# Queries loaded four tokens to a row, in a linear-attention and Fourier-mixing kernel

## The chip, the cores and the metric

The kernel runs on one core of a Trainium2 chip. The metric is the device time of one execution in microseconds (us); lower is better. A core has TensorE (PE, with its weight loads PEld), VectorE (DVE), ScalarE (ACT), GpSimd (POOL) and SyncE (SP), and sixteen DMA engines that all queues share.

## The reference

Four batches, eight heads, 768 tokens, a head dimension of 48. First comes attention with a decaying state per head (r is the query, k the key, v the value), then a mixing of the result by Fourier transforms over tokens and features, a normalisation and two dense layers (384 to 1,536 to 384).

```python
for t in range(S):
    cur = einsum('bhd,bhe->bhde', u * k_t, v_t)
    y[:, :, t] = einsum('bhd,bhde->bhe', r_t, state + cur)
    state = w[None, :, :, None] * state + einsum('bhd,bhe->bhde', k_t, v_t)
...
u = x + real(fft(fft(x, axis=1), axis=2))      # x: y with the heads side by side
un = (u - mean(u)) / sqrt(var(u) + 1e-06)
return u + relu(un @ w_ch1) @ w_ch2
```

## The kernel before

**Tiles.** The tokens of a batch are cut into six chunks of 128, so there are 24 chunks, numbered 0 to 23, six to a batch. A chunk has 128 tokens on the partitions.

**Attention of a chunk (`attend`).** `load` brings k, r and v from memory into float32 tiles: kr holds k in its first half and r in its second, eight heads of 48 each; vt holds v. Each of the three is one DMA with rows of 48 numbers (192 bytes). KR (L302, DVE) multiplies k and r by a table of decays by token, wtab, and writes them as bfloat16 into a tile whose heads are padded from 48 to 64 columns. For chunks below `TURNED` = 15, eight transposes on PE (tp, L316) turn KR, and one copy KRT, on ACT (L325) or DVE (L326), brings the result out of PSUM; from chunk 15 on a DMA transpose does both. From KRT come PR (key times query, L327), the scores A (L337), which are masked (AC and MA, on ACT with POOL, or on DVE with the table mtri), the state S (u at L369, times the decay WD), and yd, which collects the chunk's result; X is the chunk's output.

**Fourier part and dense layers.** When a batch's six X are there, HH, EO and XF fold them, matmuls with the cosine and sine tables te and hid do the transforms, UF and UB hold the sum and its normalised form, and UNT its transpose. A batch has two halves of three blocks. For each half `mlp1` makes twelve matmul groups hp (L678) with the eviction HT on ACT (L683) or DVE (L686), and `mlp2` makes three output blocks mo of twelve matmuls (L698), in two half blocks of six; osb (L705) adds the input and SP stores the block.

**Order.** Nothing is scheduled on the chip: each operation is an entry with a number, a choice of engines and a due priority, and `ORDER`, a long list of numbers written into the file, tells in which order they are emitted and (".1") that the second engine of the choice is taken. Each engine works through its own entries in that order and waits where its data is late. The list interleaves the dense layers of one batch with the attention of the next. At the start PE gets fillers (idle, L203), matmuls on zeros.

**Queues.** SP issues every load of k, r (but that of chunk 0, which ACT issues) and v, the tables te, hid, ident, mtri, the DMA transposes and the stores. POOL issues the two dense weights in three parts each. kr and vt have four buffers.

**Start.** DVE zeroes the five KR tiles whole, the states, and WD, which is a table of 128 x 384 numbers in two versions. ACT takes the logarithm of w (lw) and makes the three wtab by exponentials, for the three places that a chunk can have in its half batch.

Of the kernel before, what the change touches and what calls it, by code (L numbers as in the profile page):

```python
# [27 lines left out]
def _tables():  # L28
# [18 lines left out]
    mtri = np.triu(np.ones((128, 128)), 1)  # L47
    ident = np.eye(128)
    return [np.ascontiguousarray(x.astype(bf)) for x in (te, hid, mtri, ident)]
# [43 lines left out]
118 93 135 90 108 114 110 91 137 101 117 109 95 116 111 94 102 92 98 138 136 105 0 97 129 1 107 140 96 2 112 3 132 99 113 104 4 119 5 106 120 141 6  # L93
103 121 7 139 115 122 8 212 9 124 143 10 123 214 125 142 100 11 144 215 12 13 230 14 15 146 126 217 134 127 131 213.1 232 216 218 147 222 133 224 220
233.1 16 219 225.1 17 223.1 18 149 226.1 221 235 231 130 228 234 238.1 227 150 236 240 252 19 241.1 20 21 145 229 237 128 254 239.1 242 152 22 243.1
244.1 23 255 24 148 274 246.1 245 25 247.1 257 256 209 292 276 260.1 258 264 153 277 26 248 27 249 28 29 261.1 151 259 265 253 294 278 279 295 250 262
30 266 282.1 283.1 31 154 32 280 33 251 268 267 275 263 297 210 281 211 269 284 298.1 296 155 286 314 285.1 692 287.1 699 685 156 686 293 288.1 693
948 316 300 299.1 157 290 289 302 317 700 291 301 160 304 270 303.1 318 319 305.1 306.1 158 947 706 315 707 322.1 323.1 320 308.1 307 271 309.1 273
272 324 311 687 321 708 325.1 326.1 694 701 310 328.1 327 159 313 329.1 312 695 331 702 161 330 703 688 333 689 332 696 949 697 690 704 709 691 698.1
710 711 705 34 712.1 713.1 334 715 162 721 335 716 722.1 717 727 723.1 336 163 728 729 344 718 35 36 730.1 724 735 337.1 739 353 737 736 740.1 339 738  # L100
719.1 714 953 340.1 341.1 725.1 720.1 164 741 338 753 954 742 743 726.1 950 346 342 165 754 747 755 744 969 748 343 749 167 756 761 970 750.1 765 168
762 731.1 763 766 975 764 745.1 732.1 370 977 751.1 746.1 1007 976.1 978 372 752.1 1008.1 757.1 973 373.1 347 971 733.1 758.1 974 352 979 166 972 957
345.1 734 980.1 348 1005 169 371 354 1006 388 350 170 349 958 362 959 363.1 355.1 989 172 960 406 357 990 390 171 358.1 389 359.1 963 360 173 391.1
955 964 361 965 351 956 174 1003 392 966 356 375 1004 374 176 380 981 378.1 376 951 381 983 433 177 982.1 407 398 377 379.1 759.1 967 984 179 432 364
968 393 180 365 399.1 995 396.1 394.1 397.1 952 434 996 395.1 416 961 366 417.1 435.1 1001 962 760 368 367 436 437 1002 369 408 438.1 440 439.1 382
175 993 441 409.1 383 991 384 994.1 178 985 992.1 386 454 411 385 412.1 414 413.1 986 415 387 456 987 182 400 457 1033 472 183 401 490 1034 181 410
455 459 1035 402 474 185 460.1 462 997 473.1 404 475 458 186 403 998 463 405 1036 508 418 184 492 419 491 999 420 464 1045 188 461.1 465.1 476 988
422.1 421 525 477 423.1 187 482 442 424 483.1 1009 425 1000 443 493 426 190 500 1046 427 478 193 480 428 1010 444 1047 510 431 446.1 445 501 1021 509
479 1011 1048 447.1 526 196 494 517 449 466 495 448 467 430 1022 451 498.1 496 1012 450 518.1 429 527 453 771 452 767 768 1023 468 769 772 773 770
499.1 534 189 775 497 470.1 774 469 191 776 572.1 777 471.1 779 783 780 778 781 511 484 192 782 512 481 535 485 785 513 486 515.1 516.1 194 791 784.1  # L110
786 797 787 514 792.1 1024 488.1 798 799 487 793.1 529 788.1 806 800 195 794.1 807.1 818 489.1 550 819.1 808.1 805 519 812 571 820.1 37 813 520 810.1
814 197 521 580 38 198 532 789 811.1 523.1 809.1 815 522 39 821.1 524.1 588 826 530 502 40 551 581 533 503 816.1 1013 801 199 1037 528 552 817.1 1014
790 504 802 1017 795 1038 1015 822.1 1018.1 506 505 796 573 1039 589 531 823.1 507 1016 1019 605 1040 536 1020 1049 200 824.1 1065 803 1050 606.1 597
607 825 804 1077 1066 598 537 1025 1078 1067 553 1026 201 538 1053 1068 614 554 1054 203 540 615 1027 555.1 557 556.1 539 1043 1028 574 204 1063 558
1044.1 575 541 1064 206 1029 578 542 1061 576 590 608 559 543 1030 1041 560 1062 609 561 1042.1 207 1031 610 202 544 563 1079 1032 622 1073 1080 1055
1074 205 545 1075 1056 546 1069 547 208 1076 639 562 624 1057 564 579 664 612 1070 623 565 592 611 1071 1051 548 1072 582 1058 566 1052 641 549 583
595 567 568 1093 569 570 1059 584 1094 1060 625 586 827 828 577 1095 829 839 840 830 596 841 1096 593.1 594.1 585 835 640 613 836 842.1 837 665 831
832 587 833 1081 834 838.1 843 845 844 1082 846 847 848.1 849.1 857 1083 631 858 616 850.1 859 632.1 1084 851 866 666 852 853 617 860 872 618 867 626
868 873 854 878 629.1 627.1 874 620 648 869 865 619 879 1117 880 875 855.1 881.1 1118 621 886 870.1 856.1 642 628.1 882.1 633 871.1 1105 667 634 861.1
883.1 630.1 635 1106 862.1 863.1 1119 876.1 637 591 1120 636 864 877.1 884.1 1085 638 1101 885 1086 1107 599 1102 668 649 1108 600 1121 601 669.1 671  # L120
670.1 1145 1122 1087 603 1146 602 1091 1088 672 604 643 1092 650 646.1 644.1 647.1 1097 651 652 1113 645.1 1098 1109 1114 654 653 1111 1110 655 1103
1112 656 673 1104 657 1099 674 1089 675 1100.1 1115 1090 658 677 1135 1116 659 676 1141 1136 678 660 679 1142 680 662 682 1129 663 681 661 684 1130
683 1143 887 888 1144 1131 889 891 892 890 893 1132 899 900 894 901 895 896 902.1 897 1125 898 903 1151 1126 904 905 1152 911 906 907 912.1 917 913.1
908.1 1127 918 919 1147 1128 914.1 926 920.1 1148 1139 927 928 925 932 1140 938 933 934 929 1149 939 940 1153 935 930.1 941.1 909 1154 946 1150 931.1
915 936.1 910 916 1133 942.1 1155 937.1 1137 921 1134 1156 943.1 1157 1138 922 1161 1158 1175 944.1 1162 945 1187 1176 1173 1188 1193 923 1174.1 1199
1194.1 1197 924 1200 1217 1198 1207 1218 1163 1208 1223 1164 1169 1224 1123 1170.1 1211 1124 1181 1212 1177 1182 1178 1195 1179 1189 1196 1180 1190
1221 1191 1209 1222.1 1192 1205 1210.1 1171 1206 1219 1172 1183 1220 1185 1184 1233 1186 1159 1237 1160 1234 1238 1235 1236 1201 1239 1240 1165 1166
1202 1167 1168 1225 1203 1204 1213 1229 1226 1214 1227 1228 1230 1215 1216 1231 1232
# [8 lines left out]
def kernel(  # L137
# [18 lines left out]
    te_n, hid_n, mtri_n, id_n = _tables()  # L156
# [6 lines left out]
    mtri = cp.tile([128, 128], BF16, name="mtri")  # L163
    wrow = cp.tile([128, DM], F32, name="wrow")
# [7 lines left out]
    wtab = [cp.tile([128, 2, DM], F32, name=f"wtab{i}") for i in range(3)]  # L172
    lwc = cp.tile([128, NP], F32, name="lwc")
    wdec = cp.tile([128, NP], F32, name="wdec")
    WD = [cp.tile([128, NP, 2, D], F32, name=f"WD{i}") for i in range(2)]
# [16 lines left out]
    TURNED = 15  # L192
# [16 lines left out]
    def prelude():  # L209
        def dve(ns, fn, r, w, pri):  # L210
            op(w, "DVE", ns + MEMSET, fn, r=r, w=[w], pri=pri)
# [4 lines left out]
        op("wrow", "ACT", 430, lambda: nc.scalar.dma_start(out=wrow, in_=w.rearrange("h d -> (h d)").partition_broadcast(128)),  # L216
# [18 lines left out]
        for i in range(NB):  # L235
            dve(490, lambda i=i: nc.vector.memset(KRs[i], 0.0), [], ("KR0", i), -895 + i if i < 3 else -745 + i)
        dve(60, lambda: nc.vector.memset(eps_t, 1e-6 * DM * DM), [], "eps", -800)
        dve(60, lambda: nc.vector.memset(UW, 0.0), [], "UW0", -800)
        for i in range(2):
            dve(380, lambda i=i: nc.vector.memset(WD[i], 0.0), [], ("WD0", i), -800 + 60 * i)  # L240
            dve(140, lambda i=i: nc.vector.memset(XFs[i][:, :, :, 4 * CH:], 0.0), [], ("XF0", i), -700)
# [3 lines left out]
        act(520, lambda: nc.scalar.activation(lw, wrow, Act.Ln), ["wrow", "lntab"], "lw", -895)  # L245
        for j in range(3):
            act(600, lambda j=j: nc.scalar.activation(wtab[j][:, 0, :], lw, Act.Exp, scale=ncol[:, j:j + 1]),
                ["lw", "ncol"], ("wt", j, 0), -894 + 50 * j)
            act(600, lambda j=j: nc.scalar.activation(wtab[j][:, 1, :], lw, Act.Exp, scale=icol[:, j:j + 1]),
                ["lw", "icol"], ("wt", j, 1), -893 + 50 * j)  # L250
# [41 lines left out]
    def attend(i):  # L292
# [20 lines left out]
        def transposes():  # L313
            for s in range(2):
                for p in range(NP):
                    nc.tensor.transpose(tp()[:, s, p, :], KR()[:, s, p, :], ident)  # L316
# [467 lines left out]
```

## Time and profile before

| what | value |
|---|---|
| runs shown | 182.89, 180.6, 182.84 us; median 182.84 |
| profiled execution | 182.89 us, span on the chip 180.9 us |
| PE busy | 164.0 us (91% of the span) |
| DVE busy | 141.4 us (78%) |
| ACT busy | 117.3 us (65%) |
| POOL busy | 46.8 us (26%) |
| loads of k, r and v | 24 each of 192 KB, 4.3, 4.1 and 4.1 us from issue to landing (median) |

The busy times are of one execution and overlap one another. They are means over a span whose parts differ, so the rows in 40 slices and the windows say more than the shares. "Landing" is the moment when the last part of a transfer has arrived.

### The profile page before, as it was taken

The page shows a single profiled execution, that of the slowest core. Times are in us where ns is not written, and L with a number is a line of the kernel's source. Part 1 is how long each engine was busy: PE and PEld are TensorE (multiplying, and loading weights), DVE is VectorE, ACT ScalarE, POOL GpSimd, SP SyncE. Part 2 cuts the span into 40 slices and gives each one's busy share as a digit, 9 for nine tenths or more (in the row PEclk, how much of TensorE's full clock was granted, in tenths as well). Part 3 has the DMA queues.
Part 4 walks back from the last instruction along what each step waited for, and adds up shares of the span by engine and source line. Part 5 has one row for each costly group of instructions (what it writes and reads, how often), then busy time and mean ns, then how long its engine had stood idle before and what let it go on. Part 6 is the DMA issues. An engine that isn't in the chain of part 4 may idle for free.

```text
span 180.9 us, 4299 instructions
## 1 busy us (share of the span) xinstructions
PE 164.0 (91%) x1627; PEld 107.0 (59%) x1628; DVE 141.4 (78%) x320; ACT 117.3 (65%) x278; POOL 46.8 (26%) x66
## 2 busy tenths in 40 slices
PE   4889897989999897779889999999999999999991
PEld 1345476656676665448456566776667756666650
DVE  7699998999999878999997999997697862231312
ACT  2979892999994257449998943498744798432000
POOL 6033342033263432273423608014210000000000
PEclk9999999999999999999999999999999999999999
DMA  3999999999999799799999894284001260020223
GB/s 94 207 198 209 265 225 211 183 185 177 201 195 213 146 190 221 179 235 231 178 213 197 170 223 125 67 185 135 3 2 46 75 144 1 4 87 0 87 87 130
DMA packets 97828, 26.79 MB, mean 148 GB/s; under 512 B 92432, under 2 KB 97168, under 8 KB 97808
## 3 DMA queue, kind: packets, MB, share of 16 engines
q1 hardware_dynamic: 94480, 23.77, 62.1%
q0 software_dynamic: 2144, 2.36, 8.0%
q10 hardware_dynamic: 1184, 0.39, 0.9%
q8 instruction: 12, 0.20, 0.5%
q14 instruction: 8, 0.07, 0.1%
HBM read 20.03 MB, written 4.72 MB: 137 GB/s over the span
## 4 chain that ended last, share of the span: by engine, by line
PE 49%; DVE 26%; DMA 10%; issue 4%; ACT 4%; SPq 4%; DVEq 0%
PE mm L678 21%; PE mm L698 16%; DMA kr<-in_r_dram 8%; PE mm L546 4%; DVE KR L302 4%; DVE MA L349 3%; DMA vt<-in_v_dram 2%; DVE PR L327 2%; PE mm L586 2%; DVE XF L508 2%; SPq L283 2%; DVE EO L489 2%; DVE X L435 1%; PE A_ps L337 1%; DVE HH L495 1%
## 5 line engine op out<-in xcount | busy, mean ns | idle before, releaser
L678 PE MATMUL mm<-UNT,W 128*128 128x384 bf16 x288 | 52.9, 326 | 0.7 <-DVE HT L686 0.5
L698 PE MATMUL mm<-W,HT 128*128 128x384 bf16 x288 | 50.7, 326 | 0.5 <-DMA W<-in_moe_w_ch_dram 0.5
L683 ACT ACTIVATE HT<-mm 128x384 bf16<-128x384 f32 x81 | 38.6, 493 | 12.2 <-PE mm L678 11.8
L698 PEld LDWEIGHTS <-HT 128*128 128x128 bf16 x288 | 27.1, 98 | 17.5 <-DMA W<-in_moe_w_ch_dram 0.9
L678 PEld LDWEIGHTS <-W 128*128 128x128 bf16 x288 | 26.5, 97 | 16.8 <-issue 1.3
L414 POOL TENSOR_TENSOR TT<-V,DE 128x384 bf16<-128x384 bf16 x19 | 19.7, 1035 | 47.4 <-ACT DE L412 42.4
L705 DVE SCALAR_TENSOR_TENSOR osb<-mm,rstd,UF 128x384 f32<-128x384 f32 x24 | 14.6, 612 | 17.8 <-PE mm L698 17.8
L302 DVE TENSOR_TENSOR KR<-kr,wtab 128x768 bf16<-128x768 f32 x24 | 23.9, 998 | 3.3 <-DMA kr<-in_r_dram 2.9
L346 POOL TENSOR_SCALAR_AFFINE_SELECT MA<-AC 128x512 bf16<-128x512 bf16 x26 | 19.4, 753 | 25.1 <-ACT AC L344 22.6
L344 ACT CAST AC<-A_ps 128x512 bf16<-128x512 f32 x26 | 15.0, 590 | 3.7 <-PE A_ps L337 3.3
L203 PE MATMUL mm<-zero 128*128 128x512 bf16 x40 | 12.9, 439 | 2.6 <-DVE zero L219 2.5
L349 DVE TENSOR_TENSOR MA<-A_ps,mtri 128x512 bf16<-128x512 f32 x22 | 14.8, 682 | 0.2 <-PE A_ps L337 0.2
L310 ACT CAST V<-vt 128x384 bf16<-128x384 f32 x20 | 10.2, 519 | 5.7 <-DMA vt<-in_v_dram 5.6
L555 ACT CAST TT<-mm 97x386 bf16<-97x386 f32 x11 | 6.1, 601 | 11.7 <-PE mm L546 11.7
L546 PE MATMUL mm<-te_t,XF 128*128 128x193 bf16 x99 | 11.5, 247 | 2.3 <-DVE XF L508 1.2
L619 ACT ACTIVATE lw<-UF,sm 128x384 f32<-128x384 f32 x18 | 11.1, 617 | 1.6 <-DVE UF L599 1.4
L546 PEld LDWEIGHTS <-XF 128*128 128x128 bf16 x120 | 9.8, 98 | 3.9 <-DVE XF L508 2.3
L327 DVE TENSOR_TENSOR PR<-KRT 128x512 bf16<-128x512 bf16 x24 | 11.7, 495 | 0.0
L337 PE MATMUL A_ps<-KRT 64*128 64x128 bf16 x192 | 10.0, 219 | 1.7 <-DVE MA L349 1.1
L686 DVE TENSOR_SCALAR HT<-mm 128x384 bf16<-128x384 f32 x15 | 7.9, 550 | 3.9 <-PE mm L678 3.8
L435 DVE TENSOR_TENSOR X<-yd_ps,TT 128x384 bf16<-128x384 f32 x16 | 8.8, 548 | 2.5 <-PE yd_ps L426 2.5
L599 DVE SCALAR_TENSOR_TENSOR UF<-mm,X 128x384 f32<-128x384 f32 x19 | 10.0, 555 | 0.9 <-PE mm L586 0.7
(90 smaller groups left out, 231.3 us busy)
## 6 DMA issues: line engine op xcount, KB each, us to landing
kr<-in_k_dram SPq DMA_DIRECT2D x24, 192.0 KB, 4.3
vt<-in_v_dram SPq DMA_DIRECT2D x24, 192.0 KB, 4.1
out_dram<-osb SPq DMA_DIRECT2D x24, 192.0 KB, 1.9
kr<-in_r_dram SPq DMA_DIRECT2D x23, 192.0 KB, 4.1
W<-in_moe_w_ch_dram POOLq DMA_DIRECT2D x6, 384.0 KB, 6.9
te_t<-te_c SPq DMA_DIRECT2D x1, 579.0 KB, 5.1
hid_t<-hid_c SPq DMA_DIRECT2D x1, 288.0 KB, 3.7
wrow<-in_w_dram ACTq DMA_DIRECT2D x1, 192.0 KB, 3.8
```

Source lines behind the costliest of these rows:

```text
L203: op("idle", "PE", 216, lambda: nc.tensor.matmul(z(), lhsT=zero[:, 0:128], rhs=zero, start=True, stop=True), r=["zero"], w=[("idle", len(s ...
L302: op(("KR", i), "DVE", 960, lambda: nc.vector.tensor_tensor(out=KR().rearrange("t s p (a d) -> t (s p) a d", a=2)[:, :, :, 0:D], in0=kr(). ...
L327: op(("PR", i), "DVE", 410, lambda: nc.vector.tensor_tensor(out=PR(), in0=KRT()[:, 0], in1=KRT()[:, 1], op=AluOp.mult), r=[("KRT", i)], w= ...
L344: op(("AC", i, a), "ACT", 590, lambda: nc.scalar.copy(AC(), A_ps[a]()), r=[("A", i)], w=[("AC", i, a)], new=[AC], use=[A_ps[a]], pri=pri, ...
L346: op(("MA", i, a), "POOL", 630, lambda: nc.gpsimd.affine_select(out=MA[a](), in_=AC(), pattern=[[0, NP], [1, 128]], base=0, channel_multip ...
L349: port=True, other=[("DVE", 680, False, lambda: nc.vector.tensor_tensor(out=MA[a](), in0=A_ps[a](), in1=mtri.unsqueeze(1).to_broadcast([12 ...
L414: op(("TT", i), "POOL", 830, lambda: nc.gpsimd.tensor_tensor(out=TT(), in0=V(), in1=DE().unsqueeze(2).to_broadcast([128, H, D]), op=AluOp. ...
L546: nc.tensor.matmul(fp()[:, par, :], lhsT=lhsT[:, g * CH:g * CH + 128], rhs=rhs, start=(nb == 0 and par == 0), stop=(nb == last and par == ...
L678: nc.tensor.matmul(hp(), lhsT=W1[:, dt, ft * 128:(ft + 1) * 128], rhs=UNT()[:, :, dt, :], start=(dt == 0), stop=(dt == 2))
L683: op(("HT", hf, ft), "ACT", 495, lambda: nc.scalar.activation(out=HT()[:, ft, :], in_=hp(), func=Act.Relu, scale=-1.0), r=[("hp", hf, ft)] ...
L698: nc.tensor.matmul(mo(), lhsT=HT()[:, ft, j * 128:(j + 1) * 128], rhs=W2[:, ft, :], start=(ft == 0), stop=(ft == 11))
L705: op(("osb", hf, j), "DVE", 620, lambda: nc.vector.scalar_tensor_tensor(out=osb(), in0=mo(), scalar=rstd()[:, j:j + 1], in1=UF()[:, j, :], ...
```

## The change

1. The queries of chunks 0 to 14 (`PACKED` = 15) are loaded with four consecutive tokens of a head in one row of 192 numbers (768 bytes). The partition is then a head pair and a group of four tokens, x = 32 g + p, and the row holds four tokens for each of the two heads of a pair. Two DMAs do it, one for the even and one for the odd heads.
2. Such queries need their own decay table (`rtab`): tok, a small table of token numbers, is loaded, multiplied by the logarithms of w in the new layout (`lw2`, loaded by one more DMA), and exponentiated. It replaces the query half of wtab for these chunks; the full table stays for chunks 15 to 23.
3. KR is made in two halves: KK for the keys, KR for the queries. The copy out of PSUM is in two halves too: KT for the keys, and KRT for the queries, which puts the tokens back in order while it writes (every fourth element). Each half has its own choice of ACT or DVE.
4. Only the padding of the KR tiles is zeroed, and WD shrinks to 128 x 8 numbers that are read with a broadcast.
5. `ORDER` is a new list, for the new entries, and with it the places of many operations and their engines change: of the first-layer evictions HT 32 are on DVE (15 before) and 64 on ACT (81 before); there are 50 fillers (41 before).

```diff
-    TURNED = 15
+    TURNED, PACKED, RD = 15, 15, 560
...
-            dve(490, lambda i=i: nc.vector.memset(KRs[i], 0.0), [], ("KR0", i), ...)
+            dve(180, lambda i=i: nc.vector.memset(
+                KRs[i].rearrange("t s p (a d) -> t (s p a) d", a=2)[:, :, D:], 0.0), [], ("KR0", i), ...)
...
+        op("wr2", "ACT", 430, lambda: nc.scalar.dma_start(
+            out=lw2, in_=w.rearrange("(g a) d -> g (a d)", a=2).unsqueeze(1).to_broadcast([4, 32, 96])), ...)
+        act(320, lambda: nc.scalar.activation(lw2, lw2, Act.Ln), ["wr2", "lntab"], "lw2", -894.5)
...
+            def grown(eng, j):
+                eng.tensor_tensor(out=rtab[j], in0=lw2.unsqueeze(1).to_broadcast([128, 4, 96]),
+                                  in1=tok[:, j, :].unsqueeze(2).to_broadcast([128, 4, 96]), op=AluOp.mult)
...
-           lambda: q_.dma_start(out=kr()[:, 1], in_=r[b, :, sl, :].rearrange("h p d -> p h d")),
+        def turn():
+            if i >= PACKED:
+                q_.dma_start(out=kr()[:, 1], in_=r[b, :, sl, :].rearrange("h p d -> p h d"))
+                return
+            for a in range(2):
+                q_.dma_start(out=kr()[:, 1].rearrange("x (a j) d -> x a (j d)", a=2)[:, a, :],
+                             in_=r[b, a::2, sl, :].rearrange("g (p j) d -> g p (j d)", j=4))
...
+            op(("KK", i), "DVE", 560, lambda: nc.vector.tensor_tensor(
+                out=KR()[:, 0].rearrange("t p (a d) -> t (p a) d", a=2)[:, :, 0:D],
+                in0=kr()[:, 0], in1=wtab[ph].rearrange("t (h d) -> t h d", d=D), op=AluOp.mult), ...)
+            op(("KR", i), "DVE", 560, lambda: nc.vector.tensor_tensor(
+                out=KR()[:, 1].rearrange("x j (a d) -> x j a d", a=2)[:, :, :, 0:D],
+                in0=kr()[:, 1].rearrange("x (a j) d -> x j a d", a=2),
+                in1=rtab[ph].rearrange("x j (a d) -> x j a d", a=2), op=AluOp.mult), ...)
...
+                def keys(copy):
+                    return lambda: copy(KRT()[:, 0], tp()[:, 0])
+
+                def row(copy):
+                    return lambda: copy(KRT()[:, 1].rearrange("c g (x j) -> c j g x", j=4),
+                                        tp()[:, 1].rearrange("c j (g x) -> c j g x", g=4))
...
-            op(("S", i + 1), "DVE", 555, lambda: nc.vector.tensor_tensor(out=Sn(), in0=u_ps(), in1=d, op=AluOp.mult),
+            op(("S", i + 1), "DVE", 555, lambda: nc.vector.tensor_tensor(out=Sn(), in0=u_ps(), in1=d.unsqueeze(3).to_broadcast([128, NP, 2, D]), op=AluOp.mult),
```

On SP's queue the list of loads keeps its general order: k and r of chunks 0 to 14 with v of chunks 0 to 13, then the rest. Ahead of the scores A of chunk 14, PE's list holds 24 hp groups in both versions, and 11 mo half blocks before the change, 4 after it.

## The prediction

> **What bounds the kernel now.** I read the page first (spans, then the rows in 40 slices), then three stretches by window, then the queues and the packet records of the trace, then the timelines of SP and DVE.
>
> ```profile
> span 180.9 us, 4299 instructions
> ...
> PE 164.0 (91%) x1627; PEld 107.0 (59%) x1628; DVE 141.4 (78%) x320; ACT 117.3 (65%) x278; POOL 46.8 (26%) x66
> ...
> DVE  7699998999999878999997999997697862231312
> ...
> DMA  3999999999999799799999894284001260020223
> ```
>
> TensorE looks like the bound over the whole span, but the last row is full from the first slices to about slice 24: the kernel has two halves.
>
> ```profile
> 1.50:62.00 60.50, 54.06 (x609) 34.89 (x611) 56.21 (x128) 47.55 (x107) 20.44 (x33) 1.00 1.04 199
> 62.00:107.00 45.00, 39.85 (x445) 26.36 (x443) 40.69 (x82) 32.57 (x81) 17.52 (x19) 1.00 1.01 202
> 107.00:181.00 74.00, 70.12 (x577) 45.73 (x575) 43.90 (x109) 36.94 (x90) 8.53 (x10) 1.00 0.28 77
> ```
>
> The columns are stretch, length, PE, PEld, DVE, ACT, POOL busy, granted clock, DMA share, GB/s. Up to 107 us the DMA engines have no free time (share 1.04 and 1.01); DVE has 4.3 us free in the first 60.5; PE's 54.06 includes fillers (40 of L203, 12.9 us over the span). After 107 us PE alone is full and DMA is at 0.28. The clock is 1.00 throughout and plays no part.
>
> ```profile
> DMA packets 97828, 26.79 MB, mean 148 GB/s; under 512 B 92432, under 2 KB 97168, under 8 KB 97808
> ...
> q1 hardware_dynamic: 94480, 23.77, 62.1%
> ...
> q10 hardware_dynamic: 1184, 0.39, 0.9%
> ```
>
> Nearly all packets are the 192-byte rows of k, r and v: each of 72 loads is 8 x 128 = 1,024 of them. In the packet records a 192-byte packet takes 15 ns (mean 15.9) on its engine and a 1,536-byte one 66 ns. So a load costs 1,024 / 16 x 15.9 ns = 1.02 us of all sixteen engines. Queue q10 tells how a load is shared: it carries two transfers (wrow, 128 rows; r of chunk 0, 1,024 rows) and 1,184 - 128 - 1,024 = 32 packets more, sixteen closing packets each, which are the 4-byte packets of the records. Both transfers have 128 rows outermost at source and destination, and 128 divides by 16.
>
> ```profile
> 53.61 2.62 SPq L279 DMA_DIRECT2D kr<-in_k_dram  x1
> 56.28 3.00 SPq L283 DMA_DIRECT2D kr<-in_r_dram  x1
> 59.38 1.40 SPq L289 DMA_DIRECT2D vt<-in_v_dram  x2
> ...
> 44.63 0.96 DVE L302 TENSOR_TENSOR KR<-kr,wtab 128x768 bf16<-128x768 f32 x1 [0.25 <-DMA kr<-in_r_dram]
> ...
> 60.66 2.02 DVE L302 TENSOR_TENSOR KR<-kr,wtab 128x768 bf16<-128x768 f32 x2
> ...
> 66.66 1.62 DVE L302 TENSOR_TENSOR KR<-kr,wtab 128x768 bf16<-128x768 f32 x1 [0.84 <-DMA kr<-in_r_dram]
> ```
>
> SP spends 2.6 and 3.0 us on issues that take 0.4 us when the queue is free, and KR of chunks 9, 15 and others starts on the landing of r. So loads pace the first half; chunks 13 and 14 are through KR at 62.7 us.
>
> **The change, part by part.** The sum is made against the profiled execution, 182.89 us with a span of 180.9 (2.0 outside); the median of the runs shown is 182.84.
>
> *The packed load.* Fifteen loads of r become two DMAs each, with 128 packets of 768 bytes per DMA: 3,840 packets for 15,360. No 768-byte packet of this queue stands in the trace; on the line through 192 bytes (15 ns) and 1,536 bytes (66 ns) it takes 37 ns, and half a 1,536-byte packet, 33 ns, bounds it from below, 66 from above. What matters more is how the 256 packets are shared. Spread over sixteen engines the load costs 256 / 16 x 37 = 0.59 us, 0.43 less than now: 15 x 0.43 = 6.4 us of DMA time saved. But the source is now written as 4 heads x 32 rows x 192 elements, so its outermost dimension is 4, against 128 rows at the destination. If a transfer is shared along the outermost dimension, as the sixteen shares of 8 rows suggest, only four shares can be made: 256 / 4 x 37 = 2.37 us on four engines. The other twelve do not help, as a load has landed only when its last share has. Those four also carry their share of every k and v load, so each packed load adds 2.37 - 1.02 = 1.35 us to them: 15 x 1.35 = 20.3 us lost. The two ends are -6.4 and +20.3. I take the second: every transfer that the profile shows is cut by its outermost rows, and none shows a cut along a second dimension. The Trainium skill (DMA: Bandwidth & Descriptors, Why a DMA increments its semaphore by 16 and not by 1) states it as a rule that speaks against this change: the number of engines is the largest up to 16 that divides the slowest dimension on both sides. By it the load gets four engines, and no run here has yet shown that.
>
> *Where the 20.3 us go.* In the stretch to 62 us nothing on DMA is free to give way: weights (six loads), tables and 43 loads fill it. So KR of chunk 14 ends near 62.7 + 20.3 + 0.7 = 83.7 us; 0.7 is the second copy of w, 128 rows of 384 bytes at 22 ns on four engines, 32 each. Behind it stand k, r and v of chunks 15 to 23 on SP's queue, in the same order as before, so the rest moves too. It can win back the 45.0 - 39.85 = 5.1 us that PE stood idle in the second stretch, if its work is ready. Against that, the new order leaves more work behind chunk 14's scores (A): 4 instead of 11 second-layer half blocks (mo) are ahead of them, and 7 x 6 matmuls x 0.163 us (54 of L678 in 8.78 us on the chain) = 6.8 us. I take -3 for the balance, with -5.1 and +6.8 as ends.
>
> *DVE.* KR in two halves: 15 x (2 x 0.55 - 0.95) = +2.2 us, with 0.55 from X at L435 (128x384 from float32). Seven copies KRT of 0.685 become 10 of keys and 4 of queries; a half at the same rate is 0.42, and a query copy that writes every fourth element may run at one element a cycle, 0.68: +1.1 to +2.1. Removed: half of five zeroings of KR (0.485 each), -1.2, and the wide WD (2 x 0.378, 2 x 0.218, 2 x 0.414 to six small ones of 0.06), -1.6; added: two decay products, +1.1. In all +1.6 to +2.6, hidden under the late loads in my case and not hidden if loads come early. The Trainium skill (VectorE: DVE Perf Modes, What auto-detection actually checks) makes step 1 a condition of two elements a cycle; the row of 0.685 for 1,024 elements is that faster rate, the rule would take 0.68 for each of the 4 query copies, and this moves the sum by 1 us.
>
> *ACT, PE, prelude.* ACT's eight KRT copies (1.015 each) become 16 of 0.59 (AC's row): +1.3 in an engine that is idle 13 us of the first 60.5. Ahead of the first query table ACT now has the logarithm of the second copy of w (about 0.3) and one table of chunk 1 (0.60): the table is ready at 6.34 + 0.9 = 7.2 us for 6.34 before, while the key half of KR(0), which a load ends at 6.78, runs to 7.3: nothing, unless the tok load ahead of k(0) on SP delays it by its issue, 0.4 us. 50 fillers for 41 fill PE's idle time early. SP has 15 more issues of 0.4 us, hidden under its 2 to 3 us waits for the queue.
>
> *Sum:* 182.9 + 20.3 + 0.7 - 3 = 200.9, say 201 us. Own range: 33 ns a packet (16.4 instead of 20.3) and all 5.1 won back give 182.9 + 16.4 + 0.7 - 5.1 = 194.9; 20.3 + 0.7 + 6.8 gives 210.7.
>
> **The rivals.** *Sixteen shares, DVE takes over (181 us).* If the packed load is spread, DMA has 6.4 us to give, but DVE has only 4.3 us free in the first stretch and gets about 2.1 more to do, so at most 2.2 reach the end: 182.9 - 2.2 = 180.7. For it: DVE at 93% there. Against it: the outermost 4.
>
> *Sixteen shares, and the whole relief arrives (176.5 us).* The place is the queue up to chunk 14, the price 6.4 us of DMA time; it decides if each packed load costs under 1.02 us and the order has moved DVE's work behind the loads. 17 more of the first-layer evictions (HT) are on DVE, and if they lie in the late half, where it is busy 43.9 of 74 us, they cost it nothing. 182.9 - 6.4 = 176.5. Against it: ahead of KR of chunk 14 both orders hold nearly the same list of DVE operations.
>
> *The change does not do what it says.* It does: two DMAs of 128 packets stand in the instructions of chunks 0 to 14, so only their sharing is open.
>
> **How the numbers follow.** Four shares 0.66, sixteen with DVE as bound 0.21, sixteen with the relief at the end 0.13. Two per cent, about what a measurement of this kernel can tell from no change, is 179.2 to 186.5 us. Slower: 0.65 of the first case and 0.03 of the second (a cost of the split copies) make 0.68. Faster: 0.13 and 0.02 of the second, 0.15. Same: 0.17. The time is the likeliest case's, 201. The range for 8 in 10 is 179 to 209: 0.14 below it, 0.05 above, and the likeliest case's own is 195 to 210.
>
> **What would show it right or wrong.** Right: r landing long after k of the same chunk; KR (the query half) waiting on in_r_dram by more than 10 us in total, against 2.9 now; a mean DMA share well below 1.0 in the first stretch while loads are still waited for (four engines full, twelve partly idle); KR of chunk 14 ending near 84 us; total packets near 86,500. Wrong: r landing within 4 to 5 us of its issue, the share still at 1.0 and chunk 14 at or before 62 us; then the sharing was the mistaken step. If loads are late but the end is not, it is the step that lets the late half run in the old order.

## The result, and the profile after

The changed kernel takes 206.95 us (median; 205.41 to 208.47) against 182.87 us for the kernel before on the same chip: a ratio of 1.135, 95% interval 1.122 to 1.147. It is slower by 24 us. The forecast was 201 us with a range of 179 to 209, and the likeliest case, four shares, is the one that came. But the sum was closer than its terms, as the experiments show. (Ratios here compare undisturbed runs alone, so they are not always the quotient of the medians beside them. One point of ratio is 1.8 us.)

The page of the changed kernel: span, busy times, and the rows in 40 slices.

```profile
span 204.4 us, 4366 instructions
...
PE 172.4 (84%) x1631; PEld 112.7 (55%) x1633; DVE 149.5 (73%) x355; ACT 120.7 (59%) x279; POOL 44.6 (22%) x68
...
DVE  4479868935747879779998969998859787955222
...
PEclk9969996995879759999999999999999999999999
DMA  4566779886967679999588999543800215002322
```

Before, the DMA row was full from slice 2 on. Now it lies between 4 and 9 for sixteen slices, most often at 6 or 7, and DVE, which was nearly full too, has holes: nothing is full in the mean. The same in windows (stretch, length, PE, PEld, DVE, ACT, POOL busy, granted clock, DMA share, GB/s):

```profile
0.00:20.00 20.00, 12.90 (x95) 6.39 (x96) 12.95 (x47) 12.26 (x23) 5.44 (x12) 0.91 0.59 130
20.00:40.00 20.00, 14.95 (x184) 9.82 (x186) 16.25 (x37) 12.35 (x23) 6.49 (x12) 0.91 0.78 175
40.00:62.00 22.00, 14.62 (x149) 11.77 (x147) 12.12 (x36) 12.09 (x25) 2.99 (x5) 0.77 0.81 168
62.00:84.40 22.40, 17.22 (x189) 11.12 (x185) 18.11 (x39) 18.69 (x49) 6.81 (x11) 0.85 0.78 157
84.40:130.00 45.60, 43.00 (x451) 28.61 (x449) 40.38 (x84) 33.98 (x84) 15.98 (x20) 1.00 0.97 180
130.00:204.40 74.40, 69.73 (x577) 45.01 (x574) 49.72 (x118) 31.37 (x80) 6.92 (x9) 1.00 0.26 72
```

Nearly all of the loss, 21.7 of 23.5 us of span, lies ahead of 84.4 us, where the DMA share is 0.59 to 0.81, yet work waits for loads. That is what a transfer on four of sixteen engines looks like in a mean over sixteen. From there on the picture is nearly that of before. The chain of work that ended last shows two kinds of entries that grew (start, us, what):

```profile
39.57 8.32 DMA vt<-in_v_dram
...
61.20 1.31 ACT KRT L376
```

The load of v of chunk 6, which is still spread over sixteen engines, takes 8.3 us from issue to landing (6.2 in the kernel before). The semaphore records of the trace tell when each of its sixteen shares landed: twelve between 44.1 and 44.7 us, the other four between 47.7 and 47.9. And the copy of the queries out of PSUM takes 1.3 us, twice what the prediction gave it.

The start and the end of the late stretch on DVE:

```profile
8.15 0.55 DVE L338 TENSOR_TENSOR KR<-kr,tab 128x384 bf16<-128x384 f32 x1
10.68 0.56 DVE L342 TENSOR_TENSOR KR<-kr,rtab 128x384 bf16<-128x384 f32 x1 [1.98 <-DMA kr<-in_r_dram]
...
83.89 0.55 DVE L342 TENSOR_TENSOR KR<-kr,rtab 128x384 bf16<-128x384 f32 x1
```

L338 is the key half of KR, L342 the query half. The queries of chunk 0 come 2.5 us after its keys, and KR of chunk 14 ends at 84.4 us; before it was 62.7.

### The profile page after: what moved, and what is told of

It is laid out like the page before. It is cut to its first block, busy times and chain, and to the rows that moved or that the text cites. A ratio compares the mean times of both kernels' runs of the same rounds, so it can differ in the third digit from the quotient of the medians.

```text
span 204.4 us, 4366 instructions
## 1 busy us (share of the span) xinstructions
PE 172.4 (84%) x1631; PEld 112.7 (55%) x1633; DVE 149.5 (73%) x355; ACT 120.7 (59%) x279; POOL 44.6 (22%) x68
## 2 busy tenths in 40 slices
DMA packets 86464, 26.84 MB, mean 131 GB/s; under 512 B 77228, under 2 KB 85804, under 8 KB 86444
## 4 chain that ended last, share of the span: by engine, by line
PE 50%; DVE 19%; DMA 12%; ACT 11%; issue 4%; SPq 1%; ACTq 1%; DVEq 0%
PE mm L734 17%; PE mm L754 16%; DMA vt<-in_v_dram 6%; DMA kr<-in_r_dram 6%; ACT KRT L376 4%; PE mm L642 4%; PE mm L602 4%; DVE HH L551 2%; DVE EO L545 2%; DVE KR L331 2%; DVE KRT L376 2%; DVE MA L405 2%; DVE XF L559 2%; PE A_ps L393 2%; PE tp L358 2%
## 5 line engine op out<-in xcount | busy, mean ns | idle before, releaser
L734 PE MATMUL mm<-UNT,W 128*128 128x384 bf16 x288 | 54.8, 333 | 1.4 <-ACT UNT L692 0.7
L739 ACT ACTIVATE HT<-mm 128x384 bf16<-128x384 f32 x64 | 30.4, 499 | 24.7 <-PE mm L734 24.4
L470 POOL TENSOR_TENSOR TT<-V,DE 128x384 bf16<-128x384 bf16 x19 | 17.2, 903 | 57.5 <-ACT DE L468 40.5
L742 DVE TENSOR_SCALAR HT<-mm 128x384 bf16<-128x384 f32 x32 | 16.4, 555 | 3.7 <-PE mm L734 3.7
L358 PE MATMUL tp<-ident,KR 128*128 128x128 bf16 x120 | 11.4, 243 | 7.7 <-DVE KR L342 2.9
L376 ACT COPY KRT<-tp 128x512 bf16<-128x512 bf16 x11 | 14.4, 1308 | 5.1 <-DVE KRT L373 4.9
L211 PE MATMUL mm<-zero 128*128 128x512 bf16 x48 | 15.7, 456 | 1.6 <-DVE wuc L230 1.3
L358 PEld LDWEIGHTS <-KR 128*128 128x128 bf16 x120 | 8.7, 109 | 10.6 <-DVE KR L342 3.4
L425 PE MATMUL u_ps<-V,KR 128*128 128x96 bf16 x80 | 7.0, 213 | 7.4 <-DVE V L351 7.1
L393 PEld LDWEIGHTS <-KRT 64*128 64x128 bf16 x192 | 6.6, 99 | 12.0 <-issue 5.9
```

The lines of the kernel that those rows point to most:

```text
L211: op("idle", "PE", 216, lambda: nc.tensor.matmul(z(), lhsT=zero[:, 0:128], rhs=zero, start=True, stop=True), r=["zero"], w=[("idle", len(s ...
L376: return lambda: copy(KRT()[:, 1].rearrange("c g (x j) -> c j g x", j=4), tp()[:, 1].rearrange("c j (g x) -> c j g x", g=4))
L393: nc.tensor.matmul(A_ps[a]()[:, p, :], lhsT=KRT()[rows, 0, p, :], rhs=KRT()[rows, 1, p, :], start=(p == 0), stop=(p == NP - 1), skip_group ...
L470: op(("TT", i), "POOL", 830, lambda: nc.gpsimd.tensor_tensor(out=TT(), in0=V(), in1=DE().unsqueeze(2).to_broadcast([128, H, D]), op=AluOp. ...
L734: nc.tensor.matmul(hp(), lhsT=W1[:, dt, ft * 128:(ft + 1) * 128], rhs=UNT()[:, :, dt, :], start=(dt == 0), stop=(dt == 2))
L739: op(("HT", hf, ft), "ACT", 495, lambda: nc.scalar.activation(out=HT()[:, ft, :], in_=hp(), func=Act.Relu, scale=-1.0), r=[("hp", hf, ft)] ...
```

## Were there four shares?

The queues on the page:

```profile
DMA packets 86464, 26.84 MB, mean 131 GB/s; under 512 B 77228, under 2 KB 85804, under 8 KB 86444
...
q1 hardware_dynamic: 83760, 23.77, 52.8%
...
q10 hardware_dynamic: 540, 0.44, 0.8%
```

Queue q10 now carries wrow (128 rows), the second copy of w (4 x 32 rows), and the two DMAs of r of chunk 0 (128 rows each): 512 packets. The other 28 are closing packets, one for each share: 16 for wrow and 4 for each of the three transfers whose source has 4 outermost. SP's queue, q1, fits the same count: the 94,480 packets of before, less 14 loads of 1,024 + 16, plus 28 DMAs of 128 + 4 and the tok load of 128 + 16, are 83,760. The semaphore records agree for each of the 30 packed DMAs: four updates as shares land, after a first one soon after the issue, where every load of k and v has sixteen. And between four and six packets are in progress at once for 26% of the time up to 84.4 us, against 2.5% up to 62.7 us in the kernel before. So the sharing is shown. The Trainium skill (DMA: Bandwidth & Descriptors, Why a DMA increments its semaphore by 16 and not by 1) has the rule that the number of engines is the largest up to 16 that divides the slowest dimension on both sides, and the trace agrees with it. In the packet records the 768-byte packet takes 36 ns (median, mean 39.2).

## The experiments

Theory S: the sharing of the packed load over four engines makes nearly all of the loss. Rival P: the rest of the change (split halves of KR, the reordering copy, the new order) would be slower even with well-spread loads.

A dash: that figure is not used here.

| kernel | median us | ratio to before (95%) | KR of chunk 14 ends, us |
|---|---|---|---|
| before | 182.87 | 1 | 62.7 |
| after | 206.95 | 1.135 (1.122 to 1.147) | 84.4 |
| load spread, copy with step 128 (e1_spread) | 215.01 | 1.185 (1.177 to 1.193) | 88.5 |
| copy writes consecutive elements (e2_write_rows) | 202.23 | 1.113 (1.106 to 1.120) | 82.5 |
| both repaired (e3_spread_write_rows) | 190.24 | 1.039 (1.031 to 1.048) | 68.1 |
| before, 7 loads on four engines (e4_before_four) | 195.29 | 1.074 (1.067 to 1.081) | 76.6 |
| both repaired, old order (e5_fixed_old_order) | 185.7 | 1.028 (1.021 to 1.035) | 68.6 |
| after's operations, old order (e6_broken_old_order) | 196.56 | 1.091 (1.084 to 1.097) | 79.0 |
| unpacked, new order (e7_unpacked_new_order) | 189.18 | 1.041 (1.031 to 1.051) | - |
| after with 38 fillers more (e8_more_fillers) | 209.2 | 1.158 (1.150 to 1.166) | 84.2 |
| both repaired, chunks 6 to 14 only, old order (e9_packed_6_14) | 186.96 | 1.022 (1.015 to 1.029) | 69.4 |
| the same, tables early (e10_tables_early) | 182.74 | 1.007 (1.003 to 1.011) | 65.3 |
| the same, query copies on ACT (e11_tables_early_act) | 183.87 | 1.011 (1.005 to 1.016) | - |
| both repaired, new order, v of chunk 6 early (e12_v6_early) | 192.61 | 1.054 (1.047 to 1.061) | 72.1 |

**Spread the load.** The 32 groups of four tokens are put outermost at the source. The partition becomes x = 4 p + g, so tok, the second copy of w and the query copy follow.

```diff
-                             in_=r[b, a::2, sl, :].rearrange("g (p j) d -> g p (j d)", j=4))
+                             in_=r[b, a::2, sl, :].rearrange("g (p j) d -> p g (j d)", j=4))
...
-                    return lambda: copy(KRT()[:, 1].rearrange("c g (x j) -> c j g x", j=4),
-                                        tp()[:, 1].rearrange("c j (g x) -> c j g x", g=4))
+                    return lambda: copy(KRT()[:, 1].rearrange("c g (x j) -> c j x g", j=4),
+                                        tp()[:, 1].rearrange("c j (x g) -> c j x g", g=4))
```

> The changed kernel, with the partitions of the packed queries numbered so that the source of each DMA has 32 groups of tokens outermost (then 4 head pairs, then the row of 768 bytes) in place of 4 pairs; tok, lw2 and the order in which KRT reads PSUM follow. Packets, engines and order stay. Theory S (sharing: four engines carry each packed load): each packed transfer ends in 16 closing packets instead of 4, the DMA share of the first 60 us goes back to about 1.0, chunk 14 is through KR 15 to 20 us earlier than the 84 us of the changed kernel, and the time falls by 14 to 22 us to 185 to 193. Rival C (the query copies KRT, 1.3 us each where 0.57 was planned, set the end): the loads land earlier but the time falls by under 5 us, to over 202. Rival G (the granted clock, 0.5 in 27 us of the stretch to 76 us, is a loss of its own): the time falls, but stretches at 0.5 stay.

Measured: ratio 1.185, slower than after, a miss by 20 us and more. The loads were repaired: q10 has 576 packets, 64 of them closing ones (4 x 16), and no KR waits for a load any more. But my edit had changed the copy as well. The rows of the tile KRT, after first, then this kernel (min/median/max ns; L376 copies queries, L373 keys, both 512 elements on each partition):

```profile
L376 ACT COPY KRT<-tp x11: 1284/1306/1348, 12.5 to 86.1; 128x512 bf16<-128x512 bf16 x11
L373 DVE COPY KRT<-tp x10: 388/418/426, 12.0 to 79.1; 128x512 bf16<-128x512 bf16 x10
...
L373 ACT COPY KRT<-tp x5: 585/588/673, 22.7 to 88.9; 128x512 bf16<-128x512 bf16 x5
L376 DVE COPY KRT<-tp x4: 1280/1296/1312, 15.8 to 89.6; 128x512 bf16<-128x512 bf16 x4
```

```profile
L376 ACT COPY KRT<-tp x11: 2422/2432/2484, 9.9 to 90.2; 128x512 bf16<-128x512 bf16 x11
...
L376 DVE COPY KRT<-tp x4: 2407/2428/2441, 14.4 to 94.8; 128x512 bf16<-128x512 bf16 x4
```

Same elements, same engines: 0.59 us (ACT) or 0.42 (DVE) for consecutive bf16 writes, 1.3 where the innermost write step is 4 elements, 2.43 where it is 128 elements. So the change has a second fault that the prediction did not have, and this run can't weigh the first.

**Turn the copy alone.** The inner loop of the same copy runs over j, so that it writes consecutive elements and jumps in its reads from PSUM; the load stays on four engines.

```diff
-                    return lambda: copy(KRT()[:, 1].rearrange("c g (x j) -> c j g x", j=4),
-                                        tp()[:, 1].rearrange("c j (g x) -> c j g x", g=4))
+                    return lambda: copy(KRT()[:, 1].rearrange("c g (x j) -> c g x j", j=4),
+                                        tp()[:, 1].rearrange("c j (g x) -> c g x j", g=4))
```

> The changed kernel, with only the query copy KRT turned round: it writes tokens in a row and reads PSUM with a step, where it read in a row and wrote every fourth element. Same bytes, same engines. Theory S: the copy may become shorter, but chunks wait for loads, so the time falls by 0 to 5 us, to 202 to 207. Rival C: the copy falls from 1.3 to about 0.6 us on both engines and the time by 15 times 0.7 or more, to under 197. If reading with a step costs the same 1.3 us, the time stays and C is left to the other runs.

```profile
L376 ACT COPY KRT<-tp x11: 577/585/655, 12.7 to 84.1; 128x512 bf16<-128x512 bf16 x11
...
L376 DVE COPY KRT<-tp x4: 674/685/692, 15.4 to 87.0; 128x512 bf16<-128x512 bf16 x4
```

These rows are of the turned copy: ACT is back at 0.585, DVE at 0.685. The ratio falls from 1.135 to 1.113, 2.2 points or 4 us (the interval of after alone is 1.3 points to each side). That is within the first theory; the rival's short copies came too, but not the time that it forecast for them. A jump in the read costs ACT nothing and DVE 0.27 us (0.685 for 0.418); a jump in the write costs both engines more. The Trainium skill bears on both halves. VectorE: DVE Perf Modes (What auto-detection actually checks) names a mode of two elements a cycle for 16-bit tensors that all have step 1 (its other mode of that rate is for copies within SBUF, and this one reads PSUM); the row of 0.685 against 0.418 agrees. SBUF — State Buffer (in Door 1: The DMA port swizzle) lets steps of up to 8 bf16 elements go free of a penalty; the rows of 1.3 us at a step of 4 do not agree, and the measurement decides.

**Both.** The spread load with a copy that writes consecutive elements (`"c j (x g) -> c g x j"` on the reading side).

> Both edits: 32 groups outermost in the source, and the query copy that writes tokens in a row. Theory S with C as the smaller part: 177 to 186 us, below the spread one alone by the 0.7 us of each of fifteen copies as far as they stand on the path (2 to 10 us). If S is wrong and C right: no faster than the turned copy alone. If the prediction's bound by VectorE holds, it does not go below 179.

Ratio 1.039, slower than the expected 177 to 186 us. Against the turned copy alone the spreading is worth 7.4 points, 13 us; KR of chunk 14 ends 14.4 us earlier (82.5 to 68.1). Its query half, with the turned copy alone and with both repairs:

```profile
81.92 0.55 DVE L342 TENSOR_TENSOR KR<-kr,rtab 128x384 bf16<-128x384 f32 x1
```

```profile
67.52 0.55 DVE L342 TENSOR_TENSOR KR<-kr,rtab 128x384 bf16<-128x384 f32 x1
```

This is the largest single part of the 24 us, but about half of them and not nearly all, as Theory S has it. 3.9 points stay, with nothing of the two faults left. The windows of this kernel and one line of DVE show where:

```profile
20.00:40.00 20.00, 15.53 (x180) 11.63 (x179) 15.90 (x43) 8.79 (x17) 6.49 (x12) 0.91 1.06 235
40.00:62.00 22.00, 17.00 (x209) 12.03 (x208) 18.40 (x44) 19.39 (x53) 8.14 (x12) 0.92 0.85 163
```

```profile
36.49 0.36 DVE L351 CAST V<-vt 128x384 bf16<-128x384 f32 x1 [3.60 <-DMA vt<-in_v_dram]
```

DMA is full again in the second stretch, but DVE stands 3.6 us for v of chunk 6: in the new order SP asks for it behind k and r of chunks 7 and 8 (at 29.7 us; 23.2 before).

**The suspected cost put into the kernel before.** Nothing but the loads of r of chunks 1, 3, ... 13: 128 rows become 124 + 4. 124 and 4 have 4 as their largest divisor up to 16.

```diff
-           lambda: q_.dma_start(out=kr()[:, 1], in_=r[b, :, sl, :].rearrange("h p d -> p h d")),
+           lambda: [q_.dma_start(out=kr()[lo:hi, 1], in_=r[b, :, q * 128 + lo:q * 128 + hi, :].rearrange("h p d -> p h d"))
+                    for lo, hi in (((0, 124), (124, 128)) if i % 2 and i < 15 else ((0, 128),))],
```

> The kernel before, with only the r loads of the seven odd chunks 1 to 13 split into 124 and 4 partitions, so that no more than 4 engines can share them evenly; packets, bytes, order and all engines' work stay. Theory S: each such load holds four engines for 1024 / 4 x 15.9 ns = 4.07 us where it held all for 1.02, 7 x 3.05 = 21 us more, and the time rises by 14 to 24 us to 197 to 207, with 4 closing packets for each of the split DMAs and stretches at a granted clock of 0.5 where PE waits. Rival C (copies) and the new order as causes: within 2 us of before, 182 to 185, as only seven more issues on SP are added.

Ratio 1.074. Same numbers, same rows of 192 bytes, seven loads on four engines: 13 us. q1 has 94,424 packets, 56 fewer than before: each split load leaves 2 x 4 closing packets for 16. What KR waits for, and a window:

```profile
  DMA kr<-in_r_dram: 13.4, 8
```

```profile
20.00:40.00 20.00, 14.04 (x157) 10.73 (x156) 13.04 (x31) 9.86 (x19) 5.82 (x11) 0.74 0.92 196
```

KR now waits 13.4 us for r, 2.9 before. Seven such loads should cost 7 x ((248 + 8) x 15.9 ns - 1.02) = 21.4 us of the four engines' time; 13.9 of it reach KR of chunk 14 (62.7 to 76.6), and about as much the end, just under the 14 to 24 us expected. So about two thirds arrive.

**Order against operations.** Three kernels fill the square: the repaired operations in the order of before, the unrepaired ones in the order of before, and unpacked queries in the new order. The first two differ in `ORDER` alone, where KK, KT and the tables stand beside the entries of before that they belong to. The third has the new list without the entries of the packed layout but for the query tables, which it still builds:

```diff
-    TURNED, PACKED, RD = 15, 15, 560
+    TURNED, PACKED, RD = 15, 0, 560
```

> The operations of the changed kernel with both repairs (32 groups outermost in the source, query copies that write tokens in a row: 190 us in the new order), but in the order of the kernel before: KK stands directly ahead of KR, KT of KRT, the new tables near those they replace. Theory O (what is left, 190 against 181, is the new order, in which v of chunk 6 and others come late): 177 to 184 us, chunk 14 through KR at 62 us or earlier. Rival D (the split copies and products on VectorE and ACT cost it): 186 to 192, with VectorE full and loads waiting in the first 60 us.

> The operations of the changed kernel without repairs, in the order of the kernel before. Theory S with the copies: the loss stays with the layout, 197 to 207 us, as four engines carry the packed loads in any order. Rival N (the new order carries the loss, and the old order hides late loads): under 190.

> The changed kernel with no chunk packed: loads of r as before, KR and KRT whole again, the second table of decays left in place unused in attention; everything else, the new order above all, as in the changed kernel (the entries of KK and KT are dropped from the list). Theory O: the new order alone costs 4 to 12 us, so 186 to 194. If it is the layout alone that costs: 180 to 184. Its difference from the changed kernel is the whole price of packing in this order.

| ratio | unpacked | packed, as changed | packed, both repaired |
|---|---|---|---|
| old order | 1 | 1.091 | 1.028 |
| new order | 1.041 | 1.135 | 1.039 |

The new order, with the query tables and the narrower zeroings and WD that this kernel keeps, costs 4.1 points (7.5 us), the packing as changed 9.1 points in the old order; together 13.2, and 13.5 was measured, so these two add. With both repairs they do not: there the new order costs only 1.1 points, and the two repairs together are worth 9.6 points in the new order and 6.3 in the old. So the 13 us of the spreading hold for the new order. The first kernel fell between its theories, the second just under the range of its first theory, the third met its own. Repaired packing is worth nothing in the new order (1.039 against 1.041) and costs 2.8 points in the old one. Part of the last is seen at the start: the first batch's last X ends at 33.5 us for 30.1. On ACT:

```profile
15.75 1.63 ACT L262 ACTIVATE tab<-lw,icol 128x384 f32<-128x384 f32 x3
17.39 1.28 ACT L274 ACT_TABLE_LOAD   x1
18.69 0.58 ACT L373 COPY KRT<-tp 128x512 bf16<-128x512 bf16 x1
```

Three more tables and the table load after them stand ahead of a KRT. That they make the 3.4 us is likely, but was not tested by itself.

**The clock.** The granted clock was 0.942 in after (0.77 between 40 and 62 us), 1.00 before. In the clock record of after it stands at 0.5 for 24 us of the first 76 (not 27, as one expectation above has it). Here 38 more fillers stand ahead of tp, A, u and y of chunks 3 to 12, in the changed kernel.

> The changed kernel with 38 fillers more (matmuls on zeros of 0.2 us), one ahead of each tp, A, u and y of chunks 3 to 12, where PE waits. Theory S: the granted clock falls to 0.5 because PE waits for loads, and costs little, since PE is not the bound there: the clock rises towards 1.0 and the time stays within 3 us of 207, or rises by the fillers that do not fall into a wait. Rival G (the halved clock is itself a good part of the loss): the time falls by 5 us or more.

The mean clock rises to 0.975, and in that stretch from 0.77 to 0.92:

```profile
40.00:62.00 22.00, 14.73 (x155) 11.07 (x152) 12.29 (x37) 12.44 (x25) 3.00 (x5) 0.92 0.80 167
```

The time does not fall (1.158 against 1.135), and KR of chunk 14 ends at 84.2 us for 84.4: it comes no earlier at the higher clock. PE is idle a third of this stretch at either clock. That late loads bring the clock down is seen in the kernel before with seven loads on four engines: only the split of these loads was changed there, and the clock fell from 1.00 to 0.74 between 20 and 40 us. As fillers take PE's time too, a small cost of the clock itself isn't excluded.

**Packing where it might pay.** The repaired layout for chunks 6 to 14, the first six as before, the old order, the query tables late on ACT.

```diff
-    TURNED, PACKED, RD = 15, 15, 560
+    TURNED, RD = 15, 560
+    PACKED = range(6, 15)
```

> The repaired packed load (32 row groups outermost at the source, query copy writing consecutive elements) for chunks 6 to 14 only; chunks 0 to 5 as in the kernel before; the order is that of the kernel before, with the query tables and their row of w put late on ACT and DVE (before the sqrt table load) so that the first 33 us have nothing new ahead of them. Theory L (loads set the end up to chunk 14): nine loads give back 9 x 0.43 = 3.9 us of DMA time, the batch-0 X ends near 30 us as in the kernel before (33.5 with all fifteen packed), KR of chunk 14 ends at 59 to 62 us and the time is 177 to 181 us against about 181. Theory D (DVE and ACT, not only the loads, set the first stretch): each packed chunk brings about 0.15 us more on DVE (two halves of KR) and a copy of its own on ACT, the relief is eaten, KR of chunk 14 ends at 63 to 67 us and the time is 182 to 186 us.

The start is that of before (X of chunk 5 at 30.6 us), but the ratio is 1.022, and KR of chunk 14 ends at 69.4 us, later than either theory has it. ACT shows a reason:

```profile
30.47 0.29 ACT L259 ACTIVATE lw<-lw 128x96 f32<-128x96 f32 x1
33.13 1.35 ACT L272 ACTIVATE rtab<-rtab 128x384 f32<-128x384 f32 x3 [2.38 <-DVE rtab L267]
34.50 1.28 ACT L275 ACT_TABLE_LOAD   x1
35.79 1.05 ACT L612 CAST TT<-mm 97x386 bf16<-97x386 f32 x2
```

I had put the tables in ACT's queue between two batches, behind a product that DVE reached late; TT, which the whole mixing layer waits for, starts on ACT at 35.8 us for 31.7. So two more kernels: the logarithm at 22 us, the products on POOL, the exponentials in a gap of ACT ahead of X of chunk 5; and the same with all nine query copies on ACT. The list of entries, by name:

```diff
-X(5), lw2, rl(0) on DVE, rl(1) and rl(2) on POOL, wt(0..2, 1), sqrttab, TT2
+tn, lw2, rl(0..2) on POOL, ..., X(4), wt(0..2, 1), ..., X(5), ..., sqrttab, TT2
```

> As the variant packed for chunks 6 to 14 only, but the logarithm of the second row of w stands on ACT right after tn (about 22 us), the three products of the query tables on POOL behind it (POOL is idle there for 2.4 us), and the three exponentials between the X of chunks 4 and 5, where ACT waits 2.05 us. In the variant before this one ACT waited 2.4 us for a product at 30.8 us and the first TT of the mixing layer began at 35.8 instead of 31.7, and X of batch 1's first chunk ended at 56.0 against 48.8. Theory P (that placement alone cost the time): TT at 31.7 to 32.5, X of chunk 6 at 49 to 51, KR of chunk 14 at 60 to 64, time lower by 4 us or more, 178 to 183. Theory D (DVE and ACT lack the time for the split copies): TT early, but KR of chunk 14 still ends after 65 and the time falls by less than 3 us, 184 to 187.

> The same with the nine query copies KRT all on ACT (0.59 each) where six of them were on DVE (0.68). Theory P: another 6 x 0.68 = 4 us are taken off DVE between 35 and 65 us, where it has nothing free; the time is 0 to 3 us under that of the variant with early tables. Theory D: ACT is then the one that is late (20 of 22 us busy in that stretch); same or up to 2 us above.

The first gives a ratio of 1.007 (1.003 to 1.011), 1.5 points (2.7 us) better than the late tables: within 2% of before, and not faster. Its window from 40 to 62 us, where loads were late before:

```profile
40.00:62.00 22.00, 21.08 (x232) 13.81 (x231) 21.96 (x51) 17.55 (x48) 7.30 (x12) 1.00 1.06 207
```

DVE has no time left (21.96 of 22; before 20.77), and KR of chunk 14 ends at 65.3 for 62.7. The time lies in the first theory's range, but KR and the size of the fall are the second's: the 3.9 us of DMA time given back do not show at the end. That DVE's lack of time is the reason is read from the window. Behind KR of chunk 14 this execution takes 114.6 us, before 118.2, so the 2.6 us lost ahead of it are won back. Moving six query copies from DVE to ACT gives 1.011, no gain either, as the second theory had it.

**The late v.** The repaired kernel in the new order, with v of chunks 6 and 7 in SP's list directly behind r of chunk 6:

```diff
-k6 r6 k7 r7 k8 r8 v6 v7 k9
+k6 r6 v6 v7 k7 r7 k8 r8 k9
```

> The kernel with both repairs (source spread over 32 row groups, query copy writing consecutive elements) in the order of the changed kernel, ratio 1.039; but in SP's list v of chunks 6 and 7 stand again right behind r of chunk 6, as in the kernel before, and no longer behind k and r of chunks 7 and 8. There V of chunk 6 waited 3.6 us for its load at 33 to 36.5 us, and the same with the unpacked loads in this order (4.4 us). Theory V (that place in the list is what the new order costs): the wait goes, KR of chunk 14 ends at 64 to 65.5 instead of 68.1, ratio 1.015 to 1.025. Theory O (the order costs in many places): the wait goes, but the time is won by something else that is late; ratio 1.03 to 1.045.

Worse: 1.054 against 1.039, above both ranges. The wait for v is gone, and DVE stands longer for what was put behind it:

```profile
36.37 0.56 DVE L338 TENSOR_TENSOR KR<-kr,tab 128x384 bf16<-128x384 f32 x1 [5.44 <-DMA kr<-in_k_dram]
```

This is k of a later chunk, which stands in DVE's list ahead of folds (XF) that PE then waits 5.2 us for. The new order is not one misplaced load; its lists fit one another, and a transfer moved alone makes another late. Where its 4.1 points lie in detail stays open.

## Why the prediction was right, and where it was not

- *Four shares.* Right, by the closing packets, by the landing of the shares and by the kernel before with seven loads so shared.
- *The packet.* 37 ns estimated, 36 (mean 39.2) measured; 86,500 packets, 86,464 measured.
- *What the sharing costs at the end: +20.3.* Mis-sized. By the prediction's own figures, going from four shares to sixteen frees 15 x (2.37 - 0.59) = 26.7 us of those four engines; 14.4 us of it reached KR of chunk 14 and 13 us the end. The step that failed is "nothing on DMA is free to give way": the DMA engines were full, but not every KR waited for them. In the trace of before r of chunk 6 landed at 26.6 us and its KR began at 32.9; for chunks 7 and 8 there were 4 to 5 us between. Lateness is first taken out of such slack. That this slack is what took the other half is argued from these times, not shown; in the repaired kernel other limits may hide a part too, as its DMA share is only 0.85 between 40 and 62 us.
- *KR of chunk 14 at 83.7.* It came at 84.4, by other terms: of the 21.7 us of delay 14.4 belong to the sharing, 1.9 to the copy, and 5.4 are left with both repaired.
- *The query copy.* Bounded at 0.42 to 0.68 us on DVE and 0.59 on ACT; it took 1.30 on DVE and 1.31 on ACT, outside both ends. The bounds came from rows that all write consecutive elements; none showed a write with a step, and the upper end should have been open. Worth 4 us.
- *The order: -3, with +6.8 as the other end.* After KR of chunk 14 the span has 120.0 us, 118.2 before: +1.8, between the ends. What the prediction missed is that the new order costs 7.5 us with unpacked loads too (query tables and new start included). "The list of loads keeps its general order" passed over v of chunk 6, now four loads later; but moving it back alone gained nothing, so where the 7.5 us arise stays open.
- *The start: nothing.* The query half of KR(0) waited until 10.68 us, 3 us later than KR of before ended. Its own load was the reason (7.56 us from issue to landing), not the tables.
- *The signs.* DMA share well below 1 with late loads: right. KR waiting for r by more than 10 us: wrong, 4.5 us in after and 6.9 with the same operations in the old order. Loads that are spread over all sixteen engines are late as well, as the shares of v of chunk 6 show, so waits appear elsewhere: 4.6 us at V for v and 7.1 us at u for V in after. With both repaired 3.6 and 5.4 us of these stay, so most of them belong to the order. With seven loads of 192-byte rows shared by four KR waited 13.4 us.
- *The rivals.* "Sixteen shares, DVE takes over" is nearest to the repaired kernel with early tables, though this packs nine chunks only and has the old order: DVE is full from 40 to 62 us, but the gain of 2.2 us did not come (182.7 us against 181.3 for before). With all fifteen chunks packed no repaired kernel came within 2% of before. "The whole relief arrives" appeared in no kernel.
- *The clock.* Given no part from a row of 1.00; it fell to 0.942 as PE waited. No gain came from raising it with fillers.

So that 201 was near 207 is in part luck: misjudged terms made up for one another. The sharing was about 7 us too dear (20.3 for 13), the copy 4 us too cheap, and the rest, the order above all, 9 us too cheap (-3 + 0.7 for the 7 us that stay with both repaired). This split goes by the new order, with the copy repaired first.

## What to carry to other kernels

Before packing rows to save packets, look at the outermost dimension on both sides of the transfer and count the closing packets of its queue: here fewer, larger packets on four engines lost to many small ones on sixteen. Where a copy must permute, let it write consecutive elements and jump in its reads, and give an operation that no row shows an open upper bound. A resource at 100% is worth its whole time only where each user waits for it: look at the slack between landing and use before a saving or a loss is taken into the sum in full.

## What was not expected of the hardware

- Copies of 512 bf16 elements from PSUM into SBUF: 0.585 us on ACT for consecutive writes, 1.31 with a write step of 4 elements, 2.43 with a step of 128; DVE 0.42, 1.30 and 2.43. With consecutive writes and reads that jump by 128 elements ACT needs 0.585 and DVE 0.685.
- Loads on four engines raise the landing of loads that are spread over all sixteen: of v of chunk 6 twelve shares landed 5.2 us after the issue and the last four 8.3 us after it, with a mean DMA share of 0.8.
